# Six Winograd pairs in the last two blocks of a fused attention and GEGLU kernel, with its sums, kv and norms moved

## The chip, the cores and the metric

One core of a Trainium2 chip runs the whole program. The metric is the device time of one execution in microseconds (us). Before the change the median of 9 executions is 301.39 us (301.24 to 301.62).

The engines are called PE (matrix multiply), PEld (its weight loads), DVE (vector), ACT (activation), POOL (GpSimd) and SP (here a queue that issues DMAs). Each works through its own queue in order. [...]

## The reference, cut to what matters

```python
# q, k, v: (8 batches, 8 heads, 576 tokens, 64)
q_s = softmax(q, axis=-1)                      # over the 64 channels of a head
k_s = softmax(k, axis=2)                       # over the tokens
kv  = einsum('bhsd,bhse->bhde', k_s, v)        # 64 x 64 for each head
x   = einsum('bhsd,bhde->bhse', q_s, kv)       # attention output
x   = x.transpose(0, 2, 1, 3).reshape(4608, 512)
g, val = x @ w_gate, x @ w_val                 # 512 -> 1536
out = (gelu(g) * val) @ w_out                  # 1536 -> 512
```

## The kernel before, in words

The 4608 tokens are worked in nine blocks of 512 columns. Blocks 0 to 7 hold 512 tokens of one batch each. Block 8 holds the 64 tokens that remain of each batch (tile xtr). The order is 0 to 6, then 8, then 7. All matmuls are f16.

A block has two stages. The first, called FI below, makes the hidden tile ht: 12 chunks (fi 0 to 11) of 128 hidden channels by 512 tokens. The second, the output stage, multiplies ht with w_out.

In the output stage `out_strassen` uses a Winograd scheme with 7 products of 12 matmuls (128x256) instead of 8. It runs them in the order 1, 2, 5, 6, 3, 7, 4 in three PSUM tiles (psa, psb, psc). It needs four sums of parts of ht (`sum_h`, numbers 1 to 4): product 5 reads sum 1, product 6 sum 2, product 3 sum 4, product 7 sum 3. The last tiles of these sums are made in the output stage itself, on DVE. In block 8 the variable `late` puts product 2 near the end.

From block 3 on the FI stage is `fi_pairs`. Chunks 6 to 11 are plain: a "half" is one chunk for gate or value, 4 matmuls of 128x512. Chunks 0 to 5 are made as three pairs (0,3), (1,4), (2,5) with the same Winograd scheme on the weight side: 7 products of 4 matmuls of 128x256. One pair has four steps, which this document numbers .1 to .4:

- .1: products 1 and 5. ACT copies psum pga to pgb, and takes a scaled copy of pgc (snq).
- .2: products 6 and 3. ACT takes a scaled copy of pga, DVE adds it to pgc (cc, first half).
- .3: products 7 and 2. DVE adds the first snq to pga (cc, second half); ACT applies gelu to pgb and DVE multiplies (`final`). ACT applies gelu to cc, and POOL multiplies the two halves of cc into ht (here called the upper product).
- .4: product 4 on pga, and a `final`.

Between the steps stands one half each. The pairs need sums of weights (`sum_wgv`, DVE, made once in block 2) and sums of x (`sum_x`, POOL, four operations for each block: products 5, 6, 7 and 4 read the first to fourth).

What belongs to the next blocks rides at fixed places of a hand-written plan: `at(b, kind, i, ...)` hangs work on block b at a place, and `ride` runs it there. Kinds before are FI, NS (output stage, after a product), HF (after a half) and PR (after a pair). Riding work is: loads of q, k, v; exp of q and k (ACT); norm sums and norm products of q (DVE, POOL); the DMA transpose of q (`unit_td`, SP); the cast of v (POOL); `unit_kv4` (the product of k and v, PE and two small DVE operations); `unit_x4` (the product of q and kv, PE, copied out by ACT and DVE). A helper `big` hands out the 8 PSUM banks in a ring.

The lines of the profile that matter: L443 plain halves, L580 products of a pair, L661 products of the output stage, L593 gelu of a half, L595 its product, L601 and L602 `final`, L608 snq, L612 cc, L623 the copy to pgb, L639 gelu of cc, L640 upper product, L552 `sum_h`, L564 `sum_wgv`, L570 `sum_x`, L690 and L696 copies and adds of the output stage, L740 the copy out of product 4.

Of the kernel before, what the change touches and what calls it, by code (L numbers as in the profile page):

```python
# [18 lines left out]
def kernel(  # L19
# [86 lines left out]
    for i in range(2):  # L106
# [6 lines left out]
    ws = {nm: const.tile([P, 3, 2, NO // 2 * P], f16, name=f"ws{nm}") for nm in "gv"}  # L113
    xs = const.tile([P, 4, 2, 256], f16)
    q0r = const.tile([64, H, D], f32)
    eq0r = const.tile([P, C], f16)
    ld_b = {nm: [const.tile([P, H, NC * D], f32, name=f"{nm}t{i}") for i in range(n)]
            for nm, n in (("k", 2), ("v", 1), ("q", 1))}

# [29 lines left out]
    def load(src, nm, b, h0, h1, n0):  # L149
        tiles[(nm, b)] = ld_b[nm][b % len(ld_b[nm])]  # L150
        for t, c0 in ((0, n0), (1, 1)):
            (nc.scalar if b == 0 and t == 1 else nc.sync).dma_start(
                out=tiles[(nm, b)][t:P:2, h0:h1, c0 * D:NC * D],
                in_=src[b, h0:h1].rearrange("h (m n) d -> m h (n d)", n=NT)[
                    :, :, (4 * t + c0) * D:(4 * t + NC) * D])
# [36 lines left out]
    def exp(nm, b, h0=0, h1=H, n0=0):  # L192
        dst = ek_b[0] if nm == "k" else eq_b[b % 2]
        o, i = (("p n (c t d) -> p c t n d", "p c t (n d) -> p c t n d") if b >= QUAD else
                ("p n (h d) -> p h n d", "p h (n d) -> p h n d"))
        nc.scalar.activation(  # L196
            out=dst[:, n0:NC, h0 * D:h1 * D].rearrange(o, d=D, **({"t": 2} if b >= QUAD else {})),
            in_=heads(tiles[(nm, b)], b, h0, h1)[..., n0 * D:NC * D].rearrange(i, d=D),
            func=ACTF.Exp)
# [10 lines left out]
    def norm_sum(b, hp, n0=0):  # L210
        n = NC - n0
        e = eq_b[b % 2][:, n0:NC, hp * P:(hp + 1) * P].rearrange("p n (h d) -> p n h d", d=D)
        rq = att.tile([P, n, 2], f32, name="rq", tag="rq", bufs=4)
        nc.vector.reduce_sum(rq, e, axis=mybir.AxisListType.X)  # L214
        rrq = att.tile([P, n, 2], f32, name="rrq", tag="rrq", bufs=4)
        nc.vector.reciprocal(out=rrq, in_=rq)
        st[(b, "norm", hp)] = (e, rrq, n)

    def norm_pair(b, g, n0, engs):

        n = NC - n0
        e = eq_b[b % 2][:, n0:NC, 2 * g * P:(2 * g + 2) * P].rearrange("p n (h d) -> p n h d", d=D)
# [16 lines left out]

    def exp_rem0():  # L240
        nc.scalar.activation(out=eq0r[0:64, :].rearrange("p (h d) -> p h d", d=D), in_=q0r,
                             func=ACTF.Exp)

    def norm_rem0():
# [5 lines left out]
        nc.vector.tensor_tensor(  # L250
# [84 lines left out]
    def unit_t(b, g, eng="dve", between=()):  # L335
# [3 lines left out]
        for j in range(2):  # L339
# [3 lines left out]
            for n in range(NM):  # L343
                nc.tensor.transpose(
                    pst[:, j, n * P:(n + 1) * P],
                    eq_b[b % 2][:, n + 1, hp * P:(hp + 1) * P], ident)
# [3 lines left out]
    def unit_trem(b):  # L350

        src = eq0r[0:64] if b == 0 else eq_b[b % 2][:, 0, :]
# [6 lines left out]
    def unit_td(b):  # L359
# [3 lines left out]
                                    in_=eq_b[b % 2].rearrange("p n c -> p (n c)"))  # L363
# [192 lines left out]
    def sum_wgv(nm, i):  # L556
        w = wg_sb if nm == "g" else wv_sb
        n = NO // 2 * P
        a11, a21 = w[:, 0:2, 0:n], w[:, 0:2, n:2 * n]
        a12, a22 = w[:, 2:4, 0:n], w[:, 2:4, n:2 * n]  # L560
        t = [ws[nm][:, i] for i in range(3)]
# [4 lines left out]
    def sum_x(xt):  # L566
# [5 lines left out]
    def product_gv(i, ps, xt, k, first):  # L572
        lo, hi = slice(k * P, (k + 1) * P), slice((k + NO // 2) * P, (k + NO // 2 + 1) * P)
        for t, w, nm in ((0, wv_sb, "v"), (1, wg_sb, "g")):
            for c in range(2):
                a = {1: w[:, c, lo], 2: w[:, 2 + c, lo], 3: ws[nm][:, 2, c, lo], 4: w[:, 2 + c, hi],
                     5: ws[nm][:, 0, c, lo], 6: ws[nm][:, 1, c, lo], 7: w[:, c, hi]}[i]
# [5 lines left out]
    def fi_pairs(b, xt):  # L583
        cs = [(c, nm) for k in range(NO // 2) for c in (NO + k, NO + NO // 2 + k) for nm in "gv"]
        psg = {}

        def half(n):
            c, nm = cs[n]
            t = big([P, 512], f32, "ps" + nm)
            mm_gv(t, wg_sb if nm == "g" else wv_sb, xt, c, range(HP))  # L590
            if nm == "g":
                psg[c] = ffn.tile([P, 512], f32, name="gl", tag="gl")
                nc.scalar.activation(out=psg[c], in_=t, func=ACTF.Gelu)  # L593
            else:
                nc.vector.scalar_tensor_tensor(out=ht[:, c, :], in0=t, scalar=_H_SCALE,  # L595
                                               in1=psg[c], op0=ALU.mult, op1=ALU.mult)
            ride(b, HF, n)

        def final(ps, fi):
# [6 lines left out]
        def snap(ps):  # L606
            sn = ffn.tile([P, 2, 256], f32, name="snq", tag="snq", bufs=3)
            nc.scalar.activation(out=sn, in_=ps, func=ACTF.Copy, scale=_H_SCALE)  # L608
            return sn
# [5 lines left out]
        ride(b, HF, -1)  # L615
        half(0)
        half(1)
        for k in range(NO // 2):
            cc = ffn.tile([P, 2, 2, 256], f32, name="cc", tag="cc", bufs=1)
# [6 lines left out]
            s5 = snap(pc)  # L626
            half(3 * k + 2)
# [5 lines left out]
            half(3 * k + 3)  # L633
# [4 lines left out]
            glc = ffn.tile([P, 2, 256], f32, name="glc", tag="gl")  # L638
            nc.scalar.activation(out=glc, in_=cc[:, :, 1], func=ACTF.Gelu, scale=1.0 / _H_SCALE)  # L639
            nc.gpsimd.tensor_tensor(  # L640
                out=ht[:, k:NO:NO // 2, 256:512], in0=cc[:, :, 0], in1=glc, op=ALU.mult)
            half(3 * k + 4)
            product_gv(4, pa, xt, k, False)
            final(pa, k + NO // 2)
            if k == NO // 2 - 1:
                half(11)
            ride(b, PR, k)
# [3 lines left out]
    def product(i, ps, first, ts=(0, 1)):  # L651
        for j in range(NO):
            for t in ts:
# [5 lines left out]
                if w is None:  # L659
                    w = tw[{4: 4, 5: 1, 6: 2, 7: 3}[i]][:, j]  # L660
                nc.tensor.matmul(ps[t], a, w, start=(first and j == 0 and (  # L661
                    t == ts[0] or ps[t].tensor is not ps[ts[0]].tensor)),
                                 stop=(j == NO - 1), skip_group_check=True)
# [4 lines left out]
    def out_strassen(b, last):  # L668
# [31 lines left out]
        def second():  # L700
            get("b")
            product(2, ps["b"], True)
            add("b", s1, 0, 0)
            for x in tiles_["b"]:
                let_go(x)

        late = b == B
        get("a")
        product(1, ps["a"], True)
        s1 = snap("a")  # L710
        if not late:
            second()
        sum_h(*last_js(b), (4,))
        get("c")
        product(5, ps["c"], True)
        if not late:
            sum_h(*last_js(b), (3,))
        s5 = snap("c")
        if late:
            sum_h(*last_js(b), (3,))  # L720
        product(6, ps["a"], False)
        s2 = snap("a")
        ride(b, NS, 2)
        product(3, ps["c"], False)
        add("c", s2, 0, 1)
        for x in tiles_["c"]:
            let_go(x)
        if not late:
            store_rows(b, 0, yo[0])
# [3 lines left out]
        product(7, ps["a"], False)  # L733
        add("a", s5, 1, 1)
        ride(b, NS, 4)
        if late:
            second()
            store_rows(b, 0, yo[0])
        product(4, ps["a"], False)
# [101 lines left out]
    FI, NS, HF, PR = range(4)  # L841
# [7 lines left out]
    def load_2nd():  # L849
        load_batch(2, ((q, "q"), (k, "k")))  # L850
        for h0 in (0, 4):
            nc.sync.dma_start(out=q0r[:, h0:h0 + 4], in_=q[0, h0:h0 + 4].rearrange(
                "h (m n) d -> m h (n d)", n=NT)[:, :, 0:D])
# [37 lines left out]
    at(2, FI, 5, L(unit_kv4, 3), L(cast_v, 4, 0, H), L(sum_wgv, "g", 1))  # L891
    at(2, FI, 6, L(sum_wgv, "g", 2))
    at(2, FI, 9, L(sum_wgv, "g", 4))
    at(2, FI, 11, L(sum_wgv, "g", 3))
    at(2, NS, 2, L(sum_wgv, "v", 1), L(sum_wgv, "v", 2))
    at(2, FI, NFI - 1, L(exp, "q", 4), L(exp, "k", 4), exp_rem0)
    at(3, HF, 8, L(norm_rem0))
    at(3, HF, 11, L(unit_trem, 0))
    for b in range(3, B):
        n = b + 1  # L900
        if n < B:
            at(b, HF, -1, L(norm_sum, n, 0), L(norm_mul, n, 0, "pool"), L(norm_sum, n, 1),
               L(norm_mul, n, 1, "pool"))
            at(b, HF, 1, L(norm_sum, n, 2), L(norm_mul, n, 2, "pool"))
            at(b, HF, 2, L(norm_sum, n, 3), L(norm_mul, n, 3, "pool"))
            at(b, HF, 3, L(unit_td, n))
        if n + 1 < B:
            at(b, HF, 0, L(load_2, n + 1))
            at(b, HF, 5, L(cast_v, n + 1, 0, 4))
            at(b, HF, 8, L(cast_v, n + 1, 4, 8))  # L910
            at(b, HF, 11, L(exp, "q", n + 1), L(exp, "k", n + 1))
    for b in range(2, B - 1):
        n = b + 1
        at(b, NS, 4, L(unit_x4, n, ("act", "dve"), 0 if n == 4 else None))
        if n + 1 < B:
            at(b, NS, 4, L(unit_kv4, n + 1, True))
        if b == 2:
            at(b, NS, 4, L(sum_wgv, "v", 4), L(sum_wgv, "v", 3), one_ring)
        at(b, NS, 4, L(preload, ACTF.Gelu), L(lambda n: sum_x(get_xt(n)), n) if n < B - 1 else L(sum_x, xtr))
    at(B, NS, 2, L(lambda: sum_x(get_xt(B - 1))))  # L920
    for b in range(3, B + 1):
        for j in range(NO // 2 - 1):
            at(b, PR, j, L(sum_h, j, NO, (1, 2)), L(sum_h, j, NO, (3, 4), "pool"))
# [6 lines left out]
    for b in order:  # L930
# [9 lines left out]
        if b > 2:  # L940
            fi_pairs(b, xt)
# [18 lines left out]
        else:  # L960
            sum_h(*last_js(b), (1, 2))
# [31 lines left out]
```

## Time and profile before

| what | value |
|---|---|
| time, median of 9 | 301.39 us |
| the profiled execution | 301.24 us, of which its span is 299.4 us |
| granted clock of PE | 0.998 |
| PE busy | 286.8 us (96%) |
| DVE, ACT, POOL busy | 213.6, 173.2, 161.8 us |
| block 8, from the end of block 6's output to its own end | 236.6 to 266.7 us |
| block 7, to the end of its last matmul | 266.7 to 295.4 us |

A row of a timeline is: start in us, duration in us, engine, line, operation, tile written <- tiles read, sizes, and in brackets the idle time before it with what ended that. A row of a wait list is: engine, tile and line that waited <- what it waited for, then total us, number of times, longest. In the row of the 40 slices a digit is the busy share of 1/40 of the span in tenths.

### The profile page before, as it was taken

The numbers are of one execution on the slowest core, as the hardware profiler recorded it, in microseconds if no ns is written. First come the engines' busy times: TensorE is split into PE (matmuls) and PEld (weight loads), VectorE is DVE, ScalarE is ACT, GpSimd is POOL, SyncE is SP. The second block draws the span as 40 slices with busy tenths as digits, with TensorE's granted clock in tenths as the row PEclk, the third lists the DMA queues.
The fourth block names the chain that finished last, engine by engine and source line by source line (L and its number), as shares of the span: only waits on it lengthen the run. The fifth ranks groups of instructions, "written<-read, shape, count | busy, mean of one in ns | idle before, by whom it ended". The sixth has DMA issues, their size and how long they took to land. (4 is left out here: it accounts for less than half of the span.)

```text
span 299.4 us, 5905 instructions
## 1 busy us (share of the span) xinstructions
PE 286.8 (96%) x2293; PEld 188.4 (63%) x2293; DVE 213.6 (71%) x411; ACT 173.2 (58%) x269; POOL 161.8 (54%) x149
## 2 busy tenths in 40 slices
PE   3999999999999999899999999999999999899994
PEld 1444445446744586568666876687668666676683
DVE  2953479998767889786867786878687557845762
ACT  3763467777652577559656956595652465126530
POOL 1557557870336009991599359944981536803610
PEclk9999999999999999999999999999999999999999
DMA  6999999997189306960399029802140300023003
GB/s 221 372 383 389 401 390 388 330 320 211 74 268 295 71 2 227 383 102 2 126 337 241 3 112 344 247 2 99 55 78 0 122 22 0 2 62 81 0 2 140
DMA packets 54619, 51.69 MB, mean 173 GB/s; under 512 B 18496, under 2 KB 50496, under 8 KB 54592
## 3 DMA queue, kind: packets, MB, share of 16 engines
q1 hardware_dynamic: 52864, 49.49, 52.0%
q10 hardware_dynamic: 1728, 1.84, 1.9%
q8 instruction: 18, 0.29, 0.4%
q14 instruction: 9, 0.07, 0.1%
HBM read 37.75 MB, written 9.44 MB: 158 GB/s over the span
## 5 line engine op out<-in xcount | busy, mean ns | idle before, releaser
L443 PE MATMUL psg<-xt,wg_sb 128*128 128x512 f16 x264 | 69.7, 379 | 0.0
L443 PE MATMUL psv<-xt,wv_sb 128*128 128x512 f16 x264 | 69.7, 379 | 0.0
L443 PEld LDWEIGHTS <-wv_sb 128*128 128x128 f16 x288 | 28.1, 98 | 27.4 <-issue 0.2
L233 POOL TENSOR_TENSOR eq<-eq,rrq 128x640 f16<-128x640 f16 (+1 forms) x27 | 34.6, 1302 | 19.7 <-DVE rrq L226 8.0
L443 PEld LDWEIGHTS <-wg_sb 128*128 128x128 f16 x288 | 28.1, 98 | 25.3
L661 PEld LDWEIGHTS <-ht 128*128 128x128 f16 x384 | 37.2, 98 | 7.1 <-issue 0.8
L448 ACT ACTIVATE gl<-psg 128x512 f32<-128x512 f32 x36 | 21.0, 598 | 28.9 <-PE psg L443 28.8
L640 POOL TENSOR_TENSOR ht<-cc,glc 128x512 f16<-128x512 f32 x18 | 22.8, 1269 | 24.0 <-ACT glc L639 24.0
L449 DVE SCALAR_TENSOR_TENSOR ht<-psv,gl 128x512 f16<-128x512 f32 x36 | 24.2, 684 | 16.0 <-PE psv L443 13.7
L570 POOL TENSOR_TENSOR xs<-xt 128x512 f16<-128x512 f16 x10 | 12.0, 1203 | 43.1 <-ACT xt L174 43.1
L595 DVE SCALAR_TENSOR_TENSOR ht<-psv,gl 128x512 f16<-128x512 f32 x36 | 24.6, 685 | 4.5 <-PE psv L443 2.4
L593 ACT ACTIVATE gl<-psg 128x512 f32<-128x512 f32 x36 | 21.3, 591 | 7.9 <-PE psg L443 7.8
L172 POOL CAST v<-vt 128x640 f16<-128x640 f32 x26 | 19.1, 770 | 12.1 <-PE pskv L319 10.5
L661 PE MATMUL psa<-tw,ht 128*128 128x256 f16 x192 | 23.5, 273 | 0.2 <-DVE yo L696 0.2
L214 DVE TENSOR_REDUCE rq<-eq 128x10 f32<-128x640 f16 x28 | 22.2, 794 | 1.6 <-ACT eq L196 1.6
L196 ACT ACTIVATE ek<-kt 128x1280 f16<-128x1280 f32 (+1 forms) x11 | 19.1, 1748 | 5.6 <-DMA kt<-in_k_dram 4.1
L580 PEld LDWEIGHTS <-wv_sb 128*128 128x128 f16 x144 | 14.0, 98 | 12.8 <-DVE cc L612 1.9
L661 PEld LDWEIGHTS <-sh 128*128 128x128 f16 x192 | 18.7, 98 | 3.4 <-issue 1.0
L552 POOL TENSOR_TENSOR ht<-ht 128x512 f16<-128x512 f16 x12 | 16.7, 1394 | 6.5 <-DVE sh L552 6.5
L196 ACT ACTIVATE eq<-qt 128x2560 f16<-128x2560 f32 (+2 forms) x10 | 18.4, 1863 | 2.7 <-DMA qt<-in_q_dram 2.7
L601 ACT ACTIVATE glq<-pgb 128x256 f32<-128x256 f32 x18 | 6.9, 384 | 21.6 <-PE pgb L580 21.2
L612 DVE SCALAR_TENSOR_TENSOR cc<-pgc,snq 128x512 f32<-128x512 f32 x18 | 12.4, 686 | 7.5 <-ACT snq L608 7.4
(136 smaller groups left out, 566.0 us busy)
## 6 DMA issues: line engine op xcount, KB each, us to landing
out_dram<-yo SPq DMA_DIRECT2D x15, 512.0 KB, 3.4
kt<-in_k_dram SPq DMA_DIRECT2D x7, 640.0 KB, 8.3
vt<-in_v_dram SPq DMA_DIRECT2D x7, 640.0 KB, 5.4
qt<-in_q_dram SPq DMA_DIRECT2D x7, 640.0 KB, 7.0
qt<-in_q_dram SPq DMA_DIRECT2D x8, 512.0 KB, 7.5
wost<-in_moe_w_out_dram SPq DMA_DIRECT2D x6, 512.0 KB, 7.9
kt<-in_k_dram SPq DMA_DIRECT2D x6, 512.0 KB, 9.6
vt<-in_v_dram SPq DMA_DIRECT2D x6, 512.0 KB, 5.9
```

The lines of the kernel that those rows point to most:

```text
L172: nc.gpsimd.tensor_copy(out=dst, in_=src)
L196: nc.scalar.activation(out=dst[:, n0:NC, h0 * D:h1 * D].rearrange(o, d=D, **({"t": 2} if b >= QUAD else {})), in_=heads(tiles[(nm, b)], b, ...
L214: nc.vector.reduce_sum(rq, e, axis=mybir.AxisListType.X)
L233: (nc.gpsimd if eng == "pool" else nc.vector).tensor_tensor(out=e, in0=e, in1=rrq.unsqueeze(-1).to_broadcast((P, n, 2, D)), op=ALU.mult)
L443: nc.tensor.matmul(ps, w[:, ci, fi * P:(fi + 1) * P], xt[:, ci, :], start=(ci == 0), stop=(ci == HP - 1))
L448: nc.scalar.activation(out=gl, in_=psg, func=ACTF.Gelu)
L449: nc.vector.scalar_tensor_tensor(out=ht[:, fi, :], in0=psv, scalar=_H_SCALE, in1=gl, op0=ALU.mult, op1=ALU.mult)
L552: (nc.gpsimd if eng == "pool" else nc.vector).tensor_tensor(out=o, in0=a, in1=b, op=op)
L593: nc.scalar.activation(out=psg[c], in_=t, func=ACTF.Gelu)
L595: nc.vector.scalar_tensor_tensor(out=ht[:, c, :], in0=t, scalar=_H_SCALE, in1=psg[c], op0=ALU.mult, op1=ALU.mult)
L640: nc.gpsimd.tensor_tensor(out=ht[:, k:NO:NO // 2, 256:512], in0=cc[:, :, 0], in1=glc, op=ALU.mult)
L661: nc.tensor.matmul(ps[t], a, w, start=(first and j == 0 and (t == ts[0] or ps[t].tensor is not ps[ts[0]].tensor)), stop=(j == NO - 1), ski ...
```

## The change

- **Six pairs in blocks 8 and 7.** All twelve chunks are pairs: (0,3), (1,4), (2,5), (6,9), (7,10), (8,11). A table SIX gives the order; the steps of two pairs take turns. Step 4 of pair (8,11) stands in the output stage, inside product 1. The first step of block 7 stands ahead of product 4 of block 8. For pairs of chunk 6 and above the first snq is taken by DVE. The upper product of the last pair is on DVE.
- **Weight sums for the new pairs.** Eight more `sum_wgv`, two in each output stage of blocks 3 to 6. Those of the first pairs are spread differently over block 2.
- **Room for them.** The second buffers of k and q exp serve blocks up to 3 only; then they hold the weight sums, a second cc and part of q0r. A second xs lies in the buffer of v. The gelu of cc is done in place.
- **Late tiles last.** In the output stage from block 3 on the products take the chunks in the order 0, 3, 1, 4, 2, 5. The last `sum_h` 1 and 2 follow product 1 instead of standing ahead of it. The last sums 4 and 3 go to POOL. Block 8 has the same order of products as the others.
- **Sums of h later.** Sum 1 (DVE) and 3 (POOL) of a tile ride one place, sum 2 and 4 another two steps after it.
- **kv a block on.** From block 4 on `unit_kv4` of block b+1 rides in the output stage of block b, inside product 1 (place NS 0), instead of a block earlier ahead of product 4. The cast of v follows at NS 2. exp of q and k rides at place "e" in product 1.
- **Wider norm sums.** Norm sums go over two pairs of heads in one DVE operation ("a" at the start of a block, "n" after the first pair).
- **The rest of batch 0** (q0r): its two loads move from block 0 to block 4, its exp (now two ACT operations) to block 4, its norm sum to the end of block 5, its norm product from DVE to POOL ahead of that block's `sum_x`, its transpose to block 6.

```diff
-    def fi_pairs(b, xt):
...
+    THREE = ("a 6g l 6v 0.1 9g 0.2 9v 0.3 7g 0.4 n 1.1 t 7v 1.2 10g 1.3 s0 10v 1.4 2.1 u0 8g 2.2 s1"
+             " 8v 2.3 u1 11g 2.4 11v")
+    SIX = ("0.1 6.1 0.2 6.2 0.3 6.3 0.4 1.1 6.4 7.1 s0 1.2 7.2 1.3 u0 7.3 1.4 2.1 7.4 8.1 s1 2.2"
+           " 8.2 2.3 u1 8.3 2.4")
+    steps = {b: (SIX if b >= B - 1 else THREE).split() for b in range(3, B + 1)}
...
+        def upper(cc):
+            nc.scalar.activation(out=cc[:, :, 1], in_=cc[:, :, 1], func=ACTF.Gelu,
+                                 scale=1.0 / _H_SCALE)
+            (nc.vector if k == NFI - NO // 2 - 1 else nc.gpsimd).tensor_tensor(
+                out=ht[:, k:k + NO // 2 + 1:NO // 2, 256:512], in0=cc[:, :, 0], in1=cc[:, :, 1],
+                op=ALU.mult)
...
+            live[k] = [cc, pa, pb, pc, snap(pc, k >= NO)]
...
+        js = (0, 1, 2, 3, 4, 5) if b < 3 else (0, 3, 1, 4, 2, 5)
         get("a")
-        product(1, ps["a"], True)
+        product(1, ps["a"], True, js=js[:4])
+        ride(b, NS, 0)
+        if b >= B - 1:
+            pair_step(b, get_x(b), NFI - NO // 2 - 1, 4)
+        ride(b, PR, "e")
+        get("b")
+        product(1, ps["a"], False, js=js[4:])
+        sum_h(*last_js(b), (1, 2))
         s1 = snap("a")
...
+        sum_h(*last_js(b), (4,), "pool" if b > 2 else "dve")
...
+        sum_h(*last_js(b), (3,), "pool" if b > 2 else "dve")
...
+        if b == B:
+            go_on(B - 1, get_x(B - 1), 1)
+        product(4, ps["a"], False, js=js)
...
+            at(b, PR, "a", L(norm_pair, n, 0, 0, ("pool", "pool")))
+            at(b, PR, "n", L(norm_pair, n, 1, 0, ("pool", "pool")))
...
-        if n + 1 < B:
+        if b == 2:
             at(b, NS, 4, L(unit_kv4, n + 1, True))
+        if b == 5:
+            at(b, NS, 4, norm_rem0)
+        if b > 3:
+            at(b, NS, 0, L(unit_kv4, n, True))
...
-            at(b, PR, j, L(sum_h, j, NO, (1, 2)), L(sum_h, j, NO, (3, 4), "pool"))
+            at(b, PR, f"s{j}", L(sum_h, j, NO, (1,)), L(sum_h, j, NO, (3,), "pool"))
+            at(b, PR, f"u{j}", L(sum_h, j, NO, (2,)), L(sum_h, j, NO, (4,), "pool"))
+    for b, i, x in ((3, 1, "g1"), (3, 2, "g2"), (4, 1, "v1"), (4, 2, "v2"), (5, 1, "g4"), (5, 2, "v4"),
+                    (6, 1, "g3"), (6, 2, "v3")):
+        at(b, NS, i, L(sum_wgv, x[0], int(x[1]), NO, NO // 2))
```

## The prediction, made before the changed kernel had run

> **What bounds the kernel now.** I read the page's engine shares first, then PE's row of the 40 slices.
>
> ```profile
> PE 286.8 (96%) x2293; PEld 188.4 (63%) x2293; DVE 213.6 (71%) x411; ACT 173.2 (58%) x269; POOL 161.8 (54%) x149
> PE   3999999999999999899999999999999999899994
> PEclk9999999999999999999999999999999999999999
> ```
>
> PE is busy nearly everywhere at full clock (0.998). So a gain must be fewer PE columns or fewer PE waits. The waits of PE alone (total, times, longest):
>
> ```profile
> PE pga L580 <- DVE cc L612: 1.8, 2, 1.4
> PE psa L661 <- DVE sn L690: 0.8, 1, 0.8
> PE psa L661 <- DVE yo L696: 0.2, 1, 0.2
> ```
>
> The modelled end of a matmul hides part of each gap, so I also took the distances between matmul starts in the timeline. Against 0.216 us for 512 columns and 0.109 for 256, they show 1.5 and 0.6 us lost in block 3 (at 122.4 and 134.3), 0.24 in block 4 and 1.2 in block 8 (258 to 260). That is 3.5 us after the start-up. The chain that ended last gives the price of a half and of a product, 4 matmuls each:
>
> ```profile
> 266.66 0.86 PE psg L443 x4
> 268.39 0.44 PE pga L580 x4
> ```
>
> **1. Six more pairs.** A pair replaces four halves: 4 x 0.865 = 3.46 us. It costs 7 x 0.437 = 3.06 (268.39 to 269.26 holds two products). Gain 0.40 each, **-2.4** for six. [...] The rows here are 216 and 109, exactly half; I take the rows.
>
> **2. Waits that go.** Block 3 lost 2.1 us because DVE ran late: two weight sums, one of them 1.50 us long, four norm sums (0.79 and 0.22 each) ahead of the first cc, later the norm of batch 0 (0.67, 0.20, 0.70). All of these move. The wide sums: 0.79 at 640 elements and 1.22 at 1024 (block 0's row) extend to 1.50 at 1280; with a reciprocal of 0.25 one costs 1.75. One stands before the first pair instead of four narrow ones (4.0), the other behind the final of the first pair. There DVE's next cc is due 2.6 us later, so it is covered, with product 4 of the second pair due 5.2 us later. Block 8 lost 1.2 because of this (timelines of DVE and POOL):
>
> ```profile
> 257.19 0.82 DVE L552 TENSOR_TENSOR sh<-ht 128x512 f16<-128x512 f16 x1
> 258.04 1.26 DVE L552 TENSOR_TENSOR sh<-sh,ht 128x512 f16<-128x512 f16 x1
> ```
> ```profile
> 257.81 1.21 POOL L570 TENSOR_TENSOR xs<-xt,xs 128x512 f16<-128x512 f16 x1
> 258.98 1.33 POOL L570 TENSOR_TENSOR xs<-xt 128x512 f16<-128x512 f16 x1
> ```
>
> The DVE sum of 0.42 us waits until POOL's operation has ended (259.02) and ends 0.28 later. [...] In block 8 the change puts sums 4 and 3 ahead of sum_x in POOL's queue, so this collision goes. Block 4's 0.24 was for sum 4, now on POOL. Sum **-3.5**, if nothing takes its place.
>
> **3. kv moved.** kv stood between unit_x4 and product 4, 0.75 us of PE that covered the add yo which product 4 waits for. Block 6 has no kv there and shows the price: 0.16 idle, 0.23 by starts. After the change blocks 3, 4 and 5 have that wait as well: 3 x 0.2 = **+0.6**. The 0.75 itself only moves. In product 1 it needs exp k and the cast v, both made a block before; behind it on DVE are sums 1 and 2 (first needed by the last chunks of product 5, 2.6 us later) and the copy sn: covered. The exps follow the last gelu on ACT as before (4.7 us and a table load 1.28); their next customer, unit_x4, is 3 us behind.
>
> **4. Norm of batch 0.** Its product goes to POOL directly ahead of block 6's sum_x. From the end X of product 7 in block 5: DVE add until X+0.8, copies of x until X+2.1, sum 0.67 and reciprocal 0.2 until X+3.0, POOL's product about 1.15 (by the 128x512 sums; 64 partitions have no row here, so 0.7 to 1.25) until X+4.2, first sum_x until X+5.3. PE reaches product 5 at X+0.9+1.3+1.73+0.44 = X+4.4. **+0.95**, between 0.4 and 1.1.
>
> **5. Stages with six pairs.** Two pairs take turns, so PE needs 14 x 0.437 = 6.11 us a round. The operations on both sides, start to start when queued:
>
> ```profile
> 244.42 0.38 ACT L601 ACTIVATE glq<-pga 128x256 f32<-128x256 f32 x1
> 244.68 0.60 ACT L623 COPY pgb<-pga 128x512 f32<-128x512 f32 x1
> 245.20 0.60 ACT L608 ACTIVATE snq<-pgc 128x512 f32<-128x512 f32 x1
> ```
> ```profile
> 157.64 0.68 DVE L612 SCALAR_TENSOR_TENSOR cc<-pgc,snq 128x512 f32<-128x512 f32 x1
> 158.24 0.68 DVE L612 SCALAR_TENSOR_TENSOR cc<-pga,snq 128x512 f32<-128x512 f32 x1
> 158.84 0.41 DVE L602 SCALAR_TENSOR_TENSOR ht<-pgb,glq 128x256 f16<-128x256 f32 x1
> 159.17 0.68 DVE L595 SCALAR_TENSOR_TENSOR ht<-psv,gl 128x512 f16<-128x512 f32 x1
> ```
>
> ACT: glq 0.26, copy 0.52, snq 0.50, gelu of cc 0.53. DVE: 0.60 for 512 columns, 0.33 for 256, 0.35 for a sum. Loads a round: ACT 2 copies, 3 snq, 4 glq, 2 gelu = 4.6; DVE 4 cc, 1 snq, 4 finals, 2 sums = 5.0; POOL 2 upper (1.22) and sums (1.16 to 1.4) = 5.0. All under 6.11. But in the written order the queues form a loop. From the second pair's second cc (0.69, 0.06 to ACT): gelu of cc 0.53, glq 0.26, the next copy 0.52, snq 0.50, glq of the second pair 0.41, its final on DVE 0.33, snq on DVE 0.60, sum 1 0.35, three cc 1.80, final 0.33, sum 2 0.35, and again that cc. Together **6.7 us**: 0.6 more than PE. The first round is PE's; about 0.5 of slack goes first (the cc is done 0.5 before its product 4). Two later rounds give 2 x 0.6 - 0.5 = 0.7, and small waits on the way 0.1: 0.8 a block, **+1.6** for both.
>
> At the end of the stage DVE has one after the other: cc 0.60, two finals 0.67, the last upper product (f32 from SBUF, no row; 0.42 to 0.69, take 0.6), final 0.33, sums 0.8, copy sn 0.68: 3.7 us. PE reaches product 6, which waits for sn, after 4.4. [...] I take 0.5 for block 8 and 0.35 for block 7, whose sn is split between ACT and DVE: **+0.85**, between 0 and 2. Product 2 of the last chunk waits for the same finals, and is in this.
>
> **6. At nothing.** SP: q0r's two loads (6.8 us to landing) go behind k in block 4, whose exp is 15 us on; the transpose of q is issued some 2 us later, landing 8.4 us after; the exp of q that overwrites its source can wait 3 us. The weight sums in blocks 3 to 6 (0.55) stand behind the copies sn; POOL's sum 3 or casts can hold each by up to 0.7. The next copy is due 0.5 before product 7, so one may peep through: I add **+0.3**, between 0 and 1, for these and for the sums of h that meet POOL in blocks 3 to 6. If the cover went, four blocks would lose 0.5 each. The second cc, ws and xs in old buffers add no wait that I can find: their last readers are blocks back.
>
> **Sum.** -2.4 - 3.5 + 0.6 + 0.95 + 1.6 + 0.85 + 0.3 = -1.6. The profiled execution took 301.24 (span 299.4 and 1.84 around it), 0.15 below the median. So I expect 299.6 there, **299.8** as a median.
>
> **Rivals.**
> - *The loop is hidden.* ACT and DVE overlap a little more than the row distances say, or the slack of the first round reaches further. Then 1.6, 0.85 and 0.3 go: 297.0. For: every single load is below 6.11. Against: DVE's queue has no gap in that loop.
> - [...] In my schedule POOL is idle when each DVE sum of h comes up, since it waits for that very sum. If POOL is late by one operation, the sum meets an upper product (1.27) and waits 0.85 on average. One of two sums in each of the four late rounds adds 3.4: 303.2. It turns the sign from 0.4 us a round on. For: POOL at 5.0 of 6.1, rows of 0.82 and 1.26 us. Against: in blocks 4 to 7 of before no sum of h is over 0.43.
> - *The alternation doesn't run as written*: a bank of PSUM or a shared buffer orders the two pairs one after the other, so that PE waits in every step for the copy. About 0.5 us in each of 10 rounds and half rounds: 304.8.
>
> **How the numbers follow.** Chances: forecast 0.55 (own range 298.8 to 300.9), hidden loop 0.22, port 0.18, no alternation 0.05. Eight in ten: 297.0 to 302.2; it cuts half of the port case and the last, and the lower end of the hidden one. A measurement can tell about 0.2% (0.6 us) from no change. Faster by more than that (below 300.8): nearly all of the forecast, 0.50, and the hidden loop: 0.72. Slower (over 302.0): 0.17. Between: 0.11.
>
> **What would show it.** In the timeline of PE: product rows of 0.44 in turns in blocks 8 and 7, a round of 6.7 not 6.1; waits of PE L605 for ACT pgb, DVE snq or cc. Block 3 without the gap of 1.4. Near 208 us a wait of pgc for POOL xs. Waits of product 4 for yo in blocks 3 to 5. DVE sums in blocks 8 and 7 at 0.43. I am wrong if rounds last 6.1 (too high) or if sums of 0.8 and more stand there (too low).

## The result and the profile after

The changed kernel takes **299.84 us** (median of 9 runs, 299.60 to 300.21), against 301.38 for the kernel before (29 runs beside it). The ratio is 0.995 (0.9941 to 0.9958). The profiled execution took 299.84 us, its span 298.1 (before: 301.24 and 299.4). So it is 1.5 us faster by the medians and 1.4 by the two profiled executions.

The page's engine shares and two of the rows of 40 slices, of the changed kernel:

```profile
PE 287.5 (96%) x2365; PEld 195.4 (66%) x2365; DVE 217.9 (73%) x410; ACT 179.8 (60%) x287; POOL 181.8 (61%) x166
PE   3999999999999999999999999998999999999994
PEclk9999999999999999999999999999999999999999
```

PE's busy time is 0.7 us *more* than before, though it has 2.4 us less to do. The rows of PE end at modelled times, so some waiting counts as busy. The share of PE tells nothing here, and the distances between matmul starts have to do the work. The two slices with an 8 (the 17th in block 3, the 35th in block 8) are 9 now, and there is a new one, the 28th, at the start of block 6. The waits of PE (total, times, longest):

```profile
PE pgc L605 <- POOL xs L592: 0.8, 1, 0.8
PE psa L712 <- DVE yo L750: 0.5, 3, 0.2
PE pga L605 <- ACT pgb L660: 0.3, 2, 0.2
```

The waits of before, for cc in block 3 and for sn in block 8, are gone. The waits for xs and for pgb are new, and that for yo has grown from one of 0.2 to three with 0.5 together. The first of them is the norm of batch 0, seen in POOL's timeline and then in PE's:

```profile
206.05 1.04 POOL L273 TENSOR_TENSOR eq0r<-eq0r,rrq 64x512 f16<-64x512 f16 x1 [2.90 <-DVE rrq L272]
207.05 1.15 POOL L592 TENSOR_TENSOR xs<-xt 128x512 f16<-128x512 f16 x1
```
```profile
208.25 0.38 PE L605 MATMUL pgc<-xs,wsv 128*128 128x256 f16 x2 [0.80 <-POOL xs L592]
```

POOL stands idle for 2.90 us, waits for DVE's reciprocal, and does 1.04 us of norm before the first sum of x. Product 5 needs that sum 0.97 us before it is there (by starts).

Next, the stages of six pairs. The second cc of the second pair comes round once in each round; its two rows in block 8, with the last sum 1 behind them (DVE's timeline):

```profile
249.06 0.68 DVE L644 SCALAR_TENSOR_TENSOR eq<-pga,snq 128x512 f32<-128x512 f32 x1
...
255.79 0.69 DVE L644 SCALAR_TENSOR_TENSOR eq<-pga,snq 128x512 f32<-128x512 f32 x1
...
258.17 1.04 DVE L575 TENSOR_TENSOR sh<-ht 128x512 f16<-128x512 f16 x1
```

The distance is 6.73 us; in block 7 it is 6.73 as well. PE's work in a round is 6.11. (The tile is called eq because the second cc lies in an old buffer of q's exp.) The chain of waits, cut to block 7, shows the loop, first its part on DVE, then that on ACT:

```profile
274.66 0.43 DVE snq L638
275.08 0.33 DVE sh L575
275.42 0.38 DVE cc L644
...
275.93 0.68 DVE eq L644
276.61 0.60 DVE cc L644
277.21 0.33 DVE ht L631
277.55 0.33 DVE sh L575
277.88 0.61 DVE eq L644
...
278.57 0.27 ACT eq L648
...
279.11 0.37 ACT glq L630
279.48 0.24 ACT pgb L660
...
279.89 0.59 ACT snq L640
280.48 0.27 ACT glq L630
280.76 0.50 ACT pgb L660
...
281.29 0.27 PE pga L605
```

DVE's cc releases ACT's gelu of cc, then five more ACT operations follow in the order in which they were written, and only the last of them, the copy to pgb, lets PE go on with product 6. The loop closes over the last glq, which releases DVE's final and behind it the next snq. In block 8 its part on ACT takes 2.99 us (from the cc at 249.06 to DVE's final at 252.05) and its part on DVE 3.74 (to the cc at 255.79). No engine is full, yet the chain passes from one queue to the next with gaps of at most 0.27 us.

### The profile page after: what moved, and what is told of

The parts are those of the page before. It is cut to its first block, busy times and chain, and to the rows that moved or that the text cites. A ratio compares the mean times of both kernels' runs of the same rounds, so it can differ in the third digit from the quotient of the medians.

```text
span 298.1 us, 6098 instructions
## 1 busy us (share of the span) xinstructions
PE 287.5 (96%) x2365; PEld 195.4 (66%) x2365; DVE 217.9 (73%) x410; ACT 179.8 (60%) x287; POOL 181.8 (61%) x166
## 5 line engine op out<-in xcount | busy, mean ns | idle before, releaser
L466 PE MATMUL psg<-xt,wg_sb 128*128 128x512 f16 x240 | 63.6, 379 | 0.0
L466 PE MATMUL psv<-xt,wv_sb 128*128 128x512 f16 x240 | 63.5, 379 | 0.0
L471 ACT ACTIVATE gl<-psg 128x512 f32<-128x512 f32 x36 | 21.0, 598 | 29.0 <-PE psg L466 28.9
L466 PEld LDWEIGHTS <-wg_sb 128*128 128x128 f16 x240 | 23.3, 98 | 22.3
L472 DVE SCALAR_TENSOR_TENSOR ht<-psv,gl 128x512 f16<-128x512 f32 x36 | 24.2, 683 | 15.1 <-PE psv L466 12.7
L575 POOL TENSOR_TENSOR s<-ht,sh 128x512 f16<-128x512 f16 x18 | 21.9, 1217 | 7.0 <-DVE sh L575 7.0
L650 POOL TENSOR_TENSOR ht<-cc 128x512 f16<-128x512 f32 x12 | 15.4, 1285 | 16.6 <-ACT cc L648 16.5
L575 POOL TENSOR_TENSOR ht<-ht 128x512 f16<-128x512 f16 x18 | 21.5, 1197 | 5.7 <-DVE sh L575 5.7
L605 PEld LDWEIGHTS <-wg_sb 128*128 128x128 f16 x192 | 18.8, 98 | 2.2
L660 ACT COPY pgb<-pga 128x512 f32<-128x512 f32 x24 | 14.1, 587 | 9.7 <-PE pga L605 9.5
L631 DVE SCALAR_TENSOR_TENSOR ht<-pga,glq 128x256 f16<-128x256 f32 x24 | 10.1, 421 | 13.2 <-ACT glq L630 13.2
```

Source lines behind the costliest of these rows:

```text
L466: nc.tensor.matmul(ps, w[:, ci, fi * P:(fi + 1) * P], xt[:, ci, :], start=(ci == 0), stop=(ci == HP - 1))
L471: nc.scalar.activation(out=gl, in_=psg, func=ACTF.Gelu)
L472: nc.vector.scalar_tensor_tensor(out=ht[:, fi, :], in0=psv, scalar=_H_SCALE, in1=gl, op0=ALU.mult, op1=ALU.mult)
L575: (nc.gpsimd if eng == "pool" else nc.vector).tensor_tensor(out=o, in0=a, in1=b, op=op)
L605: nc.tensor.matmul(ps[:, t], a, x, start=(first and t == 0 and c == 0), stop=(c == 1), skip_group_check=True)
L631: nc.vector.scalar_tensor_tensor(out=ht[:, fi, 0:256], in0=ps[:, 0], scalar=_H_SCALE, in1=gl, op0=ALU.mult, op1=ALU.mult)
```

## The experiments

All times are medians in alternation with the kernel before on the same chip, which took 301.24 to 301.39 beside them; a difference of 0.2 us between two runs that were not measured side by side says little. "Excess" is always the distance between matmul starts, less 0.216 or 0.109 us.

**1. The norm of batch 0 behind the sums of x.** One edit of the plan:

```diff
-        if b == 5:
-            at(b, NS, 4, norm_rem0)
...
         at(b, NS, 4, L(lambda n: sum_x(get_x(n)), n if n < B - 1 else B))
+        if b == 5:
+            at(b, NS, 4, norm_rem0)
```

> The changed kernel, with one thing moved: in block 5 the norm of batch 0 (DVE sum and reciprocal, POOL product) stands behind the four sum_x of POOL instead of ahead of them. My theory: the changed kernel loses 0.97 us at 207 us, where product 5 of block 6 waits for the first sum_x, which stands behind that product in POOL's queue. Then this wait is gone and the time is about 298.9 us (0.9 to 1.0 less than 299.84). Rival: the wait only moves (to the first norm products of POOL or a later product that waits for a late DVE): 299.6 to 299.9.

298.82 us, ratio 0.9915 (0.9902 to 0.9929). The wait of pgc is gone from PE's list, nothing has come in its place, and the time is 1.02 lower. The wait of 0.97 us was worth all of itself.

**2. The snq of the second pair on ACT**, where the first pair has it:

```diff
-            live[k] = [cc, pa, pb, pc, snap(pc, k >= NO)]
+            live[k] = [cc, pa, pb, pc, snap(pc)]
```

> The changed kernel, with one thing else: in the stages of six pairs the first snq of the pairs of chunk 6 and above is taken by ACT, as for the others, not by DVE. Theory of the loop of queues (6.7 us a round in the changed kernel, 6.1 for PE): the loop now goes cc, gelu of cc, glq, copy, snq, glq, copy, snq, snq on ACT, then cc and what follows on DVE: 0.75 + 0.53 + 0.26 + 0.52 + 0.50 + 0.26 + 0.52 + 0.50, then 2.4 to the same cc: 6.3 us. The round is 0.4 shorter and the waits in blocks 8 and 7 fall from 0.9 to 0.1-0.3 each: 298.4 to 298.9 us. Rival, load: ACT is the fuller engine of the two in these stages by its own sum (5.1 of 6.1 us after this edit, 4.6 before), so giving it another 0.5 us a round costs: 300 to 301 us.

300.72 us, ratio 0.998 (0.9971 to 0.9989): 0.9 slower than the changed kernel. The time lies where the rival, ACT's load, had put it, but ACT is not full: the round is 6.97 us now (second cc at 249.62 and 256.59), and ACT is idle for 1.50 of it (0.36, 0.69 and 0.45). The mechanism of the loop held and my sum for it was wrong. Its words name two snq of ACT behind the second copy, its numbers hold only one. The new snq stands ahead of the snq of step 2, which the first cc needs:

```profile
253.50 0.42 DVE L575 TENSOR_TENSOR sh<-ht 128x512 f16<-128x512 f16 x1 [0.45 <-POOL ht L650]
254.12 0.69 DVE L644 SCALAR_TENSOR_TENSOR cc<-pgc,snq 128x512 f32<-128x512 f32 x1 [0.20 <-ACT snq L640]
```

DVE, with less to do, waits for POOL and for ACT instead; the wait for ACT ends last and is the one in the loop. It moved and grew.

**3. The sums of h where DVE is idle.** In the rows of DVE there are two gaps of 0.70 and 0.85 us in each round, while the loop runs through ACT. The sums went there:

```diff
-    SIX = ("0.1 6.1 0.2 6.2 0.3 6.3 0.4 1.1 6.4 7.1 s0 1.2 7.2 1.3 u0 7.3 1.4 2.1 7.4 8.1 s1 2.2"
-           " 8.2 2.3 u1 8.3 2.4")
+    SIX = ("0.1 6.1 0.2 6.2 0.3 6.3 0.4 1.1 6.4 7.1 1.2 7.2 1.3 7.3 s0 1.4 u0 2.1 7.4 8.1 2.2"
+           " 8.2 2.3 8.3 s1 2.4 u1")
```

> The changed kernel, with the sums of h in the stages of six pairs at other places: sum 1 and 3 behind step .3 of the second pair, sum 2 and 4 behind step .4 of the first pair, where DVE's queue has gaps of 0.7 and 0.85 us. Theory of the loop: both DVE sums (0.35 each) leave the loop, which is then 6.0 us, less than PE's 6.1: waits in blocks 8 and 7 fall from 0.9 to about 0.1 each, time 298.2 to 298.6 us. [...]

303.46 us, ratio 1.0071 (1.0059 to 1.0084). That is 3.6 us slower than the changed kernel. What the prediction's rival of 303.2 said of a sum that meets an upper product is right for this order. DVE's timeline, then POOL's:

```profile
250.38 0.98 DVE L575 TENSOR_TENSOR sh<-ht 128x512 f16<-128x512 f16 x1
...
251.62 1.16 DVE L575 TENSOR_TENSOR sh<-sh,ht 128x512 f16<-128x512 f16 x1
```
```profile
249.81 1.27 POOL L650 TENSOR_TENSOR ht<-cc 128x512 f16<-128x512 f32 x1 [3.86 <-ACT cc L648]
251.04 1.46 POOL L650 TENSOR_TENSOR ht<-eq 128x512 f16<-128x512 f32 x1
```

Each sum ends 0.28 us after the upper product beside it (251.36 after 251.08, 252.78 after 252.50) and takes 0.98 and 1.16 where it took 0.41. The gaps in DVE's queue are just the times at which POOL works: in the changed kernel they last from 250.07 to 250.77 and from 251.20 to 252.05, and POOL is busy from 249.28 to 252.90. The round itself is hardly longer (6.79). Most of the loss stands at the end of both stages: the sums, 0.98 and 1.03 long, stand ahead of the last finals there, and product 1 waits 1.23 us for ht, in either block. How much of that the order alone would have cost, with sums of 0.41, was not separated.

**4. Three pairs in blocks 8 and 7 again.** Everything else of the change stays. Chunks 9 to 11 of these two blocks then read weight rows that hold sums for pairs which are no longer made, so those chunks are not the reference's; operations and sizes are those of plain chunks.

```diff
-    steps = {b: (SIX if b >= B - 1 else THREE).split() for b in range(3, B + 1)}
+    steps = {b: THREE.split() for b in range(3, B + 1)}
...
-        if b >= B - 1:
-            pair_step(b, get_x(b), NFI - NO // 2 - 1, 4)
...
-        if b == B:
-            go_on(B - 1, get_x(B - 1), 1)
```

> The changed kernel, but blocks 8 and 7 are worked with three pairs and six plain chunks as blocks 3 to 6 (product 4 of the last pair is in its stage again, and the first step of block 7 is not ahead of product 4 of block 8). The weight sums for the other pairs are still made, and not used. My theory: PE work +2.4 us, waits of the six-pair stages (0.95 and 0.88, and 0.2 for sum_x) gone, so the pairs are worth only about half a microsecond net: 300.2 to 300.8 us. Rival: the waits are not a consequence of the pairs (they come with POOL's greater load and stay): 302.0 to 302.5 us. Rival: the pairs bring nothing: 299.8.

301.07 us, ratio 0.9989 (0.998 to 0.9998). The six pairs are worth 1.23 us, not 2.4. Without them the excess of 0.95 and 0.88 in the two stages and 0.36 behind block 8's goes, but 0.95 comes at a place where there was nearly none:

```profile
265.23 1.47 PE L712 MATMUL psa<-tw,ht 128*128 128x256 f16 x12 [0.78 <-DVE yo L750]
```

It is product 4 of block 8, which waits for the add yo. With six pairs the first step of block 7 stands between product 7 and product 4 and covers it. The sum: 299.84 + 2.4 - 2.2 + 0.9 = 300.9. So three quarters of the profit of the pairs, 0.95 of 1.23, come from this cover, and without it they would bring some 0.3. In the kernel before, product 2 near the end of block 8 was the cover; three pairs with a cover of that kind were not tried.

**5. No DVE sums in the two stages.** The sums 1 and 2 of the first two tiles are left out:

```diff
...
+            if b < B - 1:
+                at(b, PR, f"s{j}", L(sum_h, j, NO, (1,)))
+                at(b, PR, f"u{j}", L(sum_h, j, NO, (2,)))
...
```

> The changed kernel without the DVE sums 1 and 2 of the first two tiles in blocks 8 and 7 (that work is left out; POOL's sums 3 and 4 stay). If the loop of queues sets the stages of six pairs: it loses 2 x 0.33, 6.73 - 0.66 = 6.07, which is below the 6.11 of PE, so a round lasts 6.1 and the excess of 0.95 and 0.88 us falls to about 0.3 each: 298.5 (298.2 to 298.9). If instead each step waits for its own copy whatever DVE does (the alternation itself), nothing changes: 299.8.

299.14 us, ratio 0.9925 (0.9913 to 0.9937): 0.70 less, where I expected 1.3. DVE's second cc of the second pair, and a row between, which names what comes in place of the sums:

```profile
248.72 0.68 DVE L644 SCALAR_TENSOR_TENSOR eq<-pga,snq 128x512 f32<-128x512 f32 x1
...
253.62 0.69 DVE L644 SCALAR_TENSOR_TENSOR eq<-pgc,snq 128x512 f32<-128x512 f32 x1 [0.15 <-PE pgc L605]
...
255.21 0.68 DVE L644 SCALAR_TENSOR_TENSOR eq<-pga,snq 128x512 f32<-128x512 f32 x1
```

The round fell from 6.73 to 6.49 only (block 7: 6.40). DVE now comes early and waits for PE. The chain of waits says what PE waited for:

```profile
251.29 0.39 ACT glq L630
...
251.71 0.44 DVE ht L631
252.14 0.70 DVE snq L638
...
252.89 0.60 PE pgc L605 x4
```

There are two paths from DVE's snq to the second pair's cc. One goes through DVE's own queue, over sum 1 and the first pair's cc. The other goes over PE: product 3 adds to pgc and starts only when the snq has read it, and the cc needs product 3. From the snq to that cc the changed kernel takes 1.53 us (252.40 to 253.93, through the queue), this run 1.48 (252.14 to 253.62, over PE). So leaving out sum 1 brought 0.05 of its 0.33: shortening the first path leaves the second. The copy to pgb, for which product 6 waits 0.15 here, ends earlier than the snq. The excess of the two stages is 0.71 and 0.55.

**6, 7 and 9. Block 3 before, taken apart.** The kernel before had two late weight sums and four narrow norm sums on DVE ahead of the first cc. Run 6 brings back the narrow sums, run 7 the late weight sums, run 9 both:

```diff
...
+            if b == 3:
+                for x, hps in (("a", (0, 1)), ("a2", (2,)), ("a3", (3,))):
+                    for hp in hps:
+                        at(b, PR, x, L(norm_sum, n, hp), L(norm_mul, n, hp, "pool"))
...
```
```diff
...
-                       (FI, 11, "g3"), (NS, 1, "v4"), (NS, 2, "v3")):
+                       (FI, 11, "g3")):
...
             at(b, NS, 4, L(unit_kv4, n + 1, True))
+            at(b, NS, 4, L(sum_wgv, "v", 4), L(sum_wgv, "v", 3))
```

> The changed kernel with block 3's norm sums as before: four narrow ones, two ahead of the first half, one behind the first final, one in step 1. If what counts is when DVE comes to the first cc: 114.09 + 4 x 1.03 + 0.66 = 118.9, just when snq is there (118.91), so no loss: 299.9 (299.7 to 300.1). If the narrow norms were the cause of block 3's wait of before by themselves (1.5 us): 301.3.

> The changed kernel with weight sums v4 and v3 back where they were, after kv and x at the end of block 2's output, the wide norms kept. Their 2.08 us put the wide norm sum of block 3 from 114.1 to 116.2, its end to 117.95, the final to 118.6, the first cc to 119.2 instead of 118.9: about 0.3 us late, 300.1 (299.9 to 300.4). If the weight sums alone were block 3's 2.1 us of before: 301.9.

> The changed kernel with both of block 3's old loads on DVE: narrow norm sums and the late weight sums v4 and v3. Each alone cost nothing (299.88, 299.80). If what counts is the moment when DVE comes to the first cc: 113.98 + 1.93 + 4 x 1.03 + 0.6 = 120.6 against 118.8 when snq is there; some 1.4 to 1.8 late, so 301.3 (301.0 to 301.6). If block 3's wait went for another reason (the norm of batch 0, kv): 299.9.

299.88, 299.80 and 301.29 us (ratios 0.9949, 0.9949 and 1.000, the last from 0.9991 to 1.0009). Each alone costs nothing; both together cost 1.45 us and give back the wait of before:

```profile
PE pga L605 <- DVE cc L644: 1.4, 1, 1.4
```

DVE has over 2 us of slack at that place (the first cc of the changed kernel is preceded by 2.09 of waiting for ACT's snq). Either load fits into it, the two do not. In run 7 the slack can be read from the row of the first cc:

```profile
117.61 0.63 DVE L624 SCALAR_TENSOR_TENSOR ht<-psv,gl 128x512 f16<-128x512 f32 x1
118.80 0.69 DVE L644 SCALAR_TENSOR_TENSOR cc<-pgc,snq 128x512 f32<-128x512 f32 x1 [0.55 <-ACT snq L640]
```

After 1.93 us of weight sums DVE still has 0.55 to spare. My estimate of 0.3 late had one wait of the final (0.24) and some small overlaps counted as work.

**8 and 10. Five pairs.** A half gives PE 0.86 us of work for 0.5 of ACT or 0.6 of DVE, so four halves should let the loop breathe at a price of 0.4 a block. Both runs start from run 1 (298.82). Chunks 8 and 11 are plain, the last step is not in the output stage any more, and blocks 3 to 6 make weight sums for two new pairs only. Between the two runs only the order differs:

```diff
...
+    FIVE = ("0.1 6.1 0.2 6.2 0.3 6.3 0.4 1.1 6.4 7.1 8g s0 1.2 7.2 8v 1.3 u0 7.3 1.4 2.1 7.4"
+            " 2.2 s1 11g 2.3 u1 2.4 11v")
...
```
```diff
...
+    FIVE = ("0.1 6.1 0.2 6.2 0.3 6.3 0.4 1.1 6.4 7.1 8g s0 1.2 7.2 1.3 u0 7.3 1.4 2.1 7.4 8v"
+            " 2.2 s1 11g 2.3 u1 11v 2.4")
...
```

> Norm of batch 0 behind sum_x (298.82 by itself), and in blocks 8 and 7 five pairs in place of six: chunks 8 and 11 plain, their halves put into the second and third round of the alternation (no step in the output stage any more). PE has 0.40 more a block. If the loop of queues sets the rounds, a half gives it 0.86 us of PE for 0.5 us of ACT or 0.6 of DVE, so the excess of 0.95 and 0.88 us and the 0.36 of block 8's output go nearly all: 298.82 + 0.8 - 2.2 + 0.3 = 297.7 (297.4 to 298.2). If a pair is worth its 0.40 and the waits belong to something else: 299.6.

> Five pairs again, on the norm behind sum_x (298.82), with the four halves at other places: one between the first steps 1 and 2 of the second round, the others between steps 1, 2, 3 and 4 of the last pair. In the first try DVE had a product of a half inside its loop and the copy to pgb had no half of PE beside it. If the loop of queues is what costs, PE has 0.86 us to do at each of those places, so most of 2.2 us of excess goes: 298.82 + 0.8 - 2.2 + 0.4 = 297.8 (297.4 to 298.4). If five pairs are worse for another reason: 300 and more.

The first took 300.64 us (ratio 0.9975, 0.9965 to 0.9984), the second **298.23** (0.9897, 0.9881 to 0.9912), the fastest of this study. In the first, step 2 of the last pair follows at once on step 1, with only product 4 of another pair between:

```profile
251.87 0.38 PE L605 MATMUL pga<-xs,wsv 128*128 128x256 f16 x2 [0.78 <-ACT pgb L660]
```

The chain of waits that ends there goes back to the half itself:

```profile
246.74 0.86 PE psv L466 x4
247.60 0.44 PE pga L605 x4
248.04 0.45 PE pgb L605 x4
...
248.56 0.39 ACT glq L630
...
248.98 0.42 DVE ht L631
```

From there it runs over DVE's sum and second cc and ACT's gelu of cc to the copy. The half (8v) stands in PE's order ahead of products 7 and 2, whose results the final and the second cc wait for. So it makes the copy 0.86 us later instead of covering it, and PE has nothing to do meanwhile: excess 0.94 there and 0.51 in front of the last product 4, in both blocks. In the second order the same half stands between the copy and product 6:

```profile
250.05 1.03 PE L466 MATMUL psv<-xtr,wv_sb 128*128 128x512 f16 x4
251.04 0.38 PE L605 MATMUL pga<-xs,wsv 128*128 128x256 f16 x2
```

0.12 is left of the wait, 0.36 in each block in all. The sum: 298.82 + 0.8 (two pairs fewer) - 2.2 + 0.7 = 298.1, measured 298.23. My forecast of the first run failed since I counted what PE gains and did not ask what waits behind each half.

**11. The add yo in halves.** From run 1; the add that product 4 waits for becomes two operations of 256 columns, product 4 two times six matmuls:

```diff
-            for t, src in parts(nm):
+            for t, src in ([(slice(i, i + 1), tiles_[nm][0][:, i:i + 1]) for i in (0, 1)]
+                           if half and not last else parts(nm)):
...
-        product(4, ps["a"], False, js=js)
+        for i in (0, 1):
+            product(4, ps["a"], False, ts=(i,), js=js)
```

> Norm of batch 0 behind sum_x (298.82), and the last add yo of each output stage in two halves of 256 columns, with product 4 in two halves of 6 matmuls, each needing one half of the add. If product 4 in blocks 3 to 6 waits only for the length of the add (0.60 us, now 0.33): the 4 x 0.2 go: 298.1 (297.9 to 298.4). If the wait is for something else (the copies of x, the matmuls of x before): 298.8 to 298.9.

299.07 us, ratio 0.9927 (0.9915 to 0.994): 0.25 slower than run 1. Product 4's first half starts only when both adds are done (adds from 141.87 for 0.76 us, product at 142.68); both halves lie in one PSUM tile, psa. So the edit did not do what it was for. What it did was to make the add 0.07 longer, and the wait grew by 0.07 in each block (0.23 for 0.16 in block 3). That the length of the add sets this wait is thus supported, not shown; a way to shorten it was not found.

**12. The last sums 4 and 3 back on DVE**, in every output stage from block 3 on:

```diff
-        sum_h(*last_js(b), (4,), "pool" if b > 2 else "dve")
+        sum_h(*last_js(b), (4,))
...
-        sum_h(*last_js(b), (3,), "pool" if b > 2 else "dve")
+        sum_h(*last_js(b), (3,))
```

> The changed kernel with the last sums 4 and 3 of each output stage back on DVE. My account of block 8 of before: POOL's sum_x for block 7 waits for nothing, so without sums 4 and 3 ahead of it in POOL's queue it starts early and holds up the DVE sums of h, one of 1.26 us; then the copy sn and product 6 come late. If that is right, block 8 loses some 1.0 us again, blocks 3 to 6 up to 0.24 each, block 7 nothing (it has no sum_x): 301.0 (300.5 to 301.5). If the order of products and of late tiles is what freed block 8, and not POOL's queue: 299.9 to 300.2.

306.69 us, ratio 1.0163 (1.0142 to 1.0184): 6.85 slower, not 1.2. The direction and the place were right. Without sums 4 and 3 ahead of it, POOL's sum of x starts at 260.60 and runs on to 265.6; beside it and the POOL sum just ahead of it the DVE sums take 1.04, 1.26, 1.10 and 1.37 us. One of each (POOL, DVE):

```profile
260.60 1.33 POOL L592 TENSOR_TENSOR vt<-xt 128x512 f16<-128x512 f16 x1
```
```profile
260.95 1.26 DVE L575 TENSOR_TENSOR sh<-sh,ht 128x512 f16<-128x512 f16 x1
```

The waits of PE:

```profile
PE psc L712 <- DVE sn L744: 3.3, 3, 2.2
PE psa L712 <- DVE sn L744: 0.9, 1, 0.9
```

Excess over the changed kernel: 0.9, 0.3 and 0.3 in blocks 3, 4 and 5 (in block 3 sums of 0.82 and 0.88 stand beside the cast of v, which POOL works at from 135.56 for 3.11 us), 0.5 in block 7, where I had expected nothing, and in block 8 0.2 ahead of the output and 0.8 and 2.3 in it. The last 1.7 us are the clock, told below. I had sized this by the kernel before, where these two sums stood elsewhere in DVE's queue than the last sums 1 and 2. In the changed kernel all four stand behind product 1, and in block 8 all four meet POOL.

## Why the prediction was right

The forecast was 299.8 and the time is 299.84. Step by step, in us of the profiled execution:

| step | predicted | measured |
|---|---|---|
| 1. six more pairs | -2.4 | -2.4 (0.437 a product, as before) |
| 2. waits that go | -3.5 | -3.5 |
| 3. kv moved | +0.6 | +0.7 |
| 4. norm of batch 0 | +0.95 | +0.97 |
| 5. the loop, blocks 8 and 7 | +1.6 | +1.83 |
| 5. tails of the stages | +0.85 | +0.36 |
| 6. at nothing, and sums | +0.3 | +0.7 |
| sum | -1.6 | -1.35 (execution -1.4) |

That the forecast came within 0.04 us is luck: the loop was 0.2 too cheap, the tails 0.5 too dear and the last step 0.4 too cheap. The forecast of the profiled execution, 299.6, was 0.2 too low, and the 0.15 added for the median made up for it. The list also covers PE's stages alone. Outside it, start-up took 0.2 us more (product 4 of block 2 starts at 112.81, before at 112.61) and what follows the last matmul 0.3 less (its end moved by 1.11 us, the end of the execution by 1.4); the two nearly cancel, and neither was forecast.

**Step 1.** The rows held: 0.437 us a product again. But a pair is worth its 0.40 only where nothing waits. Run 4 puts the six at 1.23 net.

**Step 2.** Block 3 was told as one late queue with two loads. Runs 6, 7 and 9 show that: 0, 0 and 1.45. It also means that no part of the 1.45 belongs to either edit alone. The second wait of block 3 (0.6 at 134) was not tested by itself. For block 8 the mechanism (POOL's sum of x ahead of DVE's sums of h) holds by run 12, but its size is that of an order and not of an operation: 1.2 us in block 8 of the kernel before, 3.3 in that of this one.

**Step 3.** Product 4 starts 0.32 us late in blocks 3, 4 and 5, of which about 0.09 is there anyway between the matmuls of x and product 4. The mechanism, a lost cover, is supported by run 4 (0.95 us where nothing stands between); kv was not put back by itself.

**Step 4.** Right to 0.02 us, and shown by run 1. POOL's product took 1.04 us, where I had taken 1.15.

**Step 5.** The loop was right (6.7 against 6.73), and in both parts (2.97 on ACT and 3.76 on DVE against 2.99 and 3.74), and so was its shape: waits of pga for ACT's copy. What I had not seen is a second loop of 6.49 beside it, over product 3, so run 5 brought half of what I expected from cutting the first. The tails were too dear by 0.5. No run shows their terms of 0.5 and 0.35: measured were 0.36 behind block 8's stage and nothing behind block 7's. In block 8 a last sum 1 (at 258.17) lasts 1.04 beside POOL's sum 4 of 1.69, in block 7 one of 1.05 stands beside 1.70; product 6 waits 0.22 in block 8 and not at all in block 7.

**Step 6.** Mis-sized, and not for the reason given. What the 0.3 was for, weight sums and sums of h held up by POOL, cost PE nothing in blocks 3 to 6 (of the eight new weight sums three, at 139.82, 169.1 and 199.7, took 0.93, 1.10 and 1.09 beside POOL's casts of v, the other five 0.54 to 0.59), and two other waits were not in my list. Product 4 of the third pair waits 0.12 for cc in each of blocks 3 to 6: sum 1 of the second tile now stands between that pair's two cc in DVE's queue (130.81, 0.33 to the next row, in block 3), by my reading of the rows; it wasn't tried. And product 5 at 237 waits 0.21 for the sum of x of block 8. Together they are 0.7, near the error of the tails with the other sign.

**The rivals.** The hidden loop (297.0) fell with the round of 6.73. The rival of 303.2 did not come about, as every sum of h inside the stages takes 0.41 or 0.42: POOL is idle there, waiting for that very sum (sum 1) or for ACT's gelu of cc (sum 2). It is a near thing: sum 2 ends at 249.14 and POOL's next operation starts at 249.28, and run 3, which moves the sums by a step or two, has sums of 0.98 to 1.26. That its 303.46 is near the rival's number is chance, as most of that loss is at the ends of the stages. The DVE sums of run 3 end 0.28 us after POOL's operation, so by estimate some 0.13 of their 0.41 goes beside it. By what means POOL's operation holds up the sum, no run shows.

## What to carry to other kernels

Where no engine is full and the tensor engine still waits, write down the order of each queue and add row distances once around the loop; then look for the second loop before pricing a cut, because it sets what the cut can bring. Ask of every inserted operation what waits behind it in each queue that it enters, and put independent tensor work between a copy and the product that needs it: the same four halves made 300.64 in one order and 298.23 in another. A queue's slack belongs to all its edits together, so two that are free one by one can cost 1.45 us as a pair.

## What was not expected of the hardware

In run 12 a slower clock followed a stall. PE waited 0.88 and then 2.22 us for sn, and after that the next 16 matmuls of 256 columns came at 0.214 us in place of 0.109. The busy time by stretches (us, PE, PEld, DVE, ACT, POOL with counts, then the granted clock, DMA share and GB/s):

```profile
264.00:266.60 2.60, 0.38 (x5) 0.19 (x3) 2.60 (x4) 0.00 (x0) 1.62 (x2) 1.00 0.00 0
266.60:270.00 3.40, 3.40 (x17) 2.47 (x17) 1.20 (x2) 0.00 (x0) 0.00 (x0) 0.51 0.00 0
```

The granted clock was 0.51 for 3.4 us, which cost 1.7 us on top of the stalls. One of the five executions did not have it: its granted clock over the whole span is 1.000 (0.993 or 0.994 in the others), and it took 305.03 us, 1.7 less than the median. In the 2.60 us before the slow stretch, the first row, PE was busy for 0.38 and the clock still at 1.00. That the fifth execution kept its clock with the same program says that the program alone does not decide it; what did was not traced, and no run shows what brings the slower clock on or ends it. In the changed kernel, where no wait after the start-up is longer than 0.8, the granted clock over the whole span is 0.999.
